# Another order of steps in an attention pipeline, and the output layer's first sums one product later

## The chip, the cores and the metric

The kernel runs on one core of one Trainium2 chip. The metric is the device time of one execution in microseconds (us); the time before is 1461.8 us, the median of 3 runs (1461.47 to 1461.99). The profile was taken of one further execution, whose span is 1460.0 us with a mean granted TensorE clock of 1.000.

## What is computed

```python
# attention: batch 8, heads 8, seq 576, head_dim 64; q, k, v in fp32
scores = scale * np.matmul(q, k.transpose(0, 1, 3, 2))           # scale = 1/8
thresh = np.max(scores, axis=-1, keepdims=True) - tau
scores = np.where(scores >= thresh, scores, -1e9)
attn = np.exp(scores - max); attn = attn / (sum(attn) + 1e-9)    # (shortened)
attn_out = np.matmul(attn, v)
# bridge: (B, H, S, D) -> (B*S, H*D), 4608 tokens of 512
# feed-forward: d_model 512, d_ff 2048
h = np.maximum(x @ w_in, 0.0)
out = h * h @ w_out
```

## The kernel before

**Attention.** The 64 heads are worked two at a time (32 pairs). A pair has five blocks of query rows: t = 0 to 3 with 128 rows of each head, t = 4 with the last 64 rows of both heads side by side. So there are 160 blocks, numbered n = 5i + t. They run through a software pipeline: in `slot(n)` the scores of block n+3 are computed, the softmax of n+2 and n+1 goes on, the weights of block n-1 are transposed, and the value products of block n-2 are made. `slot` only sets the order in which instructions are given to the engines; every engine then takes its own in that order.

```python
def ahead(n, part):                      # scores of block n, in two parts
    i, t = slots[n]
    if part == 0:
        jobs[n] = scores_rest(i, t)      # K: one 128x128 product (t < 4), takes one of 2 score tiles
    else:
        scores(i, t, jobs[n])            # S: 64-row products, the two heads on two halves of the array
        jobs[n] = softmax(i, t, jobs[n])

def softmax(i, t, sc):                   # a generator: stage(n) and second(n) each run one step
    ...
    for j in range(nj):                  # nj = 2, or 1 for t = 4
        nc.vector.tensor_reduce(out=nmx[:, j : j + 1], in_=sc[:, ds(at[j], S)], axis=AXIS.X, op=ALU.max, negate=True)
        ...                              # after the last: threshold on GpSimd
        yield
    for j in range(nj):
        if j:
            yield
        nc.scalar.activation(out=w[:, ts(j, S)], in_=sc[:, ds(at[j], S)], func=AF.Exp, bias=nmx[:, j : j + 1], scale=1.0)
    for j in range(nj):
        yield
        nc.vector.scalar_tensor_tensor(  # mask, multiply, sum; last reader of the score tile
            out=w[:, ts(j, S)], in0=sc[:, ds(at[j], S)], scalar=thr[:, j : j + 1], in1=w[:, ts(j, S)],
            op0=ALU.is_ge, op1=ALU.mult, accum_out=sm[:, j : j + 1])
    nc.gpsimd.tensor_scalar(out=sm[:, 0:nj], in0=sm[:, 0:nj], scalar1=1e-9, scalar2=None, op0=ALU.add)
    yield
    nc.vector.reciprocal(out=sm[:, 0:nj], in_=sm[:, 0:nj])
    ...                                  # normalize on GpSimd

def bank(shape, name):                   # two PSUM banks, given out in turn
    return b_pool.tile(shape, FP32, tag="b", name=name)        # b_pool has bufs=2

# the three parts of transposes(n): "R", "W" and "w"
def rest():                              # R: the rest columns, into the bank of the value products just made
    pt, n_, of = pending.popleft() if pending else (bank([P, 3, P], "pvR"), 0, None)
    nc.tensor.transpose(pt[:, 1, :], w[:, ds(MAIN, P)], ident[:, :])
    then = turn_last(i + 1, pt[:, 2, :]) if t == 0 and i + 1 in turning else None
    ...
    nc.scalar.copy(xr[:, :, :], pt[:, 0:2, :])     # copies value products and rest out of the bank
    ...                                  # then(): two more ScalarE copies and two GpSimd copies

def main(j):                             # W: j = 0, w: j = 1 (w does nothing for t = 4)
    if j and t == FULL:
        return
    pt = bank([P, FULL, P], "pwT")
    for c in range(FULL):
        nc.tensor.transpose(pt[:, c, :], w[:, ds(j * (S + REST) + c * P, P)], ident[:, :])
    ...
    nc.scalar.copy(wT[:, j, :, at], pt[:, :, :])

def values(i, t):                        # V: 64-column products, the two heads on two halves
    pt = bank([P, 3, P], "pvR")
    ...
```

`turn_step(n, 0)` (q) and `turn_step(n, 1)` (k) transpose the queries and the keys of the next pair, four transposes each into a `bank`; they act only in blocks with n mod 5 = 0. Blocks -1 to 34 and 75 to 110 also convert weights from 64-bit floats (`fetch`, `convert1` to `convert6`); `sums_step` makes one GpSimd sum of weights.

**Feed-forward.** Both layers are 49 products of blocks in place of 64 (two nested levels of a seven-product scheme). `OUTER` is the order of the outer products m; inside each, `inner` makes seven inner products with a `tick` after each. Sums of operands are made beside the products of other groups: on GpSimd, or on DVE with one operand copied to PSUM by ScalarE (`sum_v`). In the last step of the hidden layer, `work` holds the sums that the output layer needs first:

```python
OUTER, INNER = (1, 2, 6, 7, 4, 5, 3), (1, 6, 2, 7, 5, 4, 3)

def also(m, at):                         # called at each tick; i is the place of m in OUTER
    ...
    spread(work.get(i, []), at)          # one product's list, spread over its seven ticks

def inner_sums(n, m):                    # sums 5, 6, 3 on GpSimd, 7 on DVE
    return [lambda o=o: inner_g(n, m, o) for o in (5, 6, 3, 7)]

def sum_v(op, out, x, y):
    c = banks.tile([P, BANK], FP32, tag="c", bufs=2, name="c")
    ...
    nc.scalar.copy(c, y)
    return lambda: op(nc.vector, out, x, c)
```

The order of `slot`, before, is the first part of the diff below.

Of the kernel before, what the change touches and what calls it, by code (L numbers as in the profile page):

```python
# [48 lines left out]
def kernel(  # L49
# [26 lines left out]
    B, H, S, D = q.shape  # L76
# [133 lines left out]
    def convert3(m):  # L210
        if m not in parts:
            return
        a = parts[m][2].bitcast(FP32)
        low, high = (0x38000000, 0x47EFFFFF)
        nc.gpsimd.tensor_scalar(
            out=a, in0=a, scalar1=as_float(high), scalar2=as_float(low), op0=ALU.min, op1=ALU.max
        )

    def convert4(m):
        if m not in parts:  # L220
            return
        lo, hi, a = parts[m]
        nc.vector.tensor_scalar(
            out=a, in0=a, scalar1=3, scalar2=0x3FFFFFFF, op0=ALU.logical_shift_left, op1=ALU.bitwise_and
        )
# [224 lines left out]
    def turn_part(n, part):  # L450

        if n < 0:
            return
        if n not in rows_of:
            transposes(n)
        rows_of[n][part]()
# [33 lines left out]
    def turn_step(n, at):  # L490
        i, left = divmod(n - TURN_AT[at], NB)
        i += 1
        if left == 0 and 0 < i < len(pairs):
            if at == 0:
                turns[i] = turn(i)
            next(turns[i])

    def values_and_load(n):

        if n < 0:  # L500
            return
        i, t = slots[n]
        values(i, t)
        if t == NB - 1:
            turned.pop(i), loaded_v.pop(i)
            if i + 2 < len(pairs):
                load_v(i + 2)
# [3 lines left out]
    def stage(n):  # L511
        if n in jobs:
            next(jobs[n], None)

    def second(n):

        if n in jobs and slots[n][1] < FULL:
            next(jobs[n], None)
# [15 lines left out]
    IN_FIRST = OUT_SUMS + 41  # L534
# [4 lines left out]
    def sums_step():  # L539
        while summing and next(summing[0], 0) == 0:  # L540
            summing.popleft()

    def ask():

        while later:
            to, from_ = later.popleft()
            nc.sync.dma_start(out=to, in_=from_)
# [7 lines left out]
    def begun(n):  # L555
        return starts.get(n)

    def slot(n):

        sums_start(n)  # L560
        ask()
        turn_part(n - 1, "w")
        convert4(begun(n - 3))
        convert3(begun(n - 2))
        stage(n + 2)
        turn_step(n, 0)
        values_and_load(n - 2)
        convert1(begun(n - 1))
        stage(n + 1)
        second(n + 1)  # L570
        turn_part(n - 1, "R")
        second(n + 2)
        sums_step()
        turn_part(n - 1, "W")
        convert6(begun(n - 4))
        stage(n + 2)
        second(n + 2)
        fetch(begun(n + 3))
        convert5(begun(n - 3))
        ahead(n + 3, 0)  # L580
        stage(n + 1)
        turn_step(n, 1)
        ahead(n + 3, 1)
        convert2(begun(n - 1))


    def inner(product, copy, temp, bank, final, tick):
# [297 lines left out]
    with tc.manual_schedule():  # L885
        with ExitStack() as stack:
            sc_pool = stack.enter_context(tc.tile_pool(name="sc", bufs=2, space=PSUM))
            b_pool = stack.enter_context(tc.tile_pool(name="b", bufs=2, space=PSUM))

            def bank(shape, name):  # L890
                return b_pool.tile(shape, FP32, tag="b", name=name)

            def keep_busy(times):

                pt = bank([P, P], "idle")
                for _ in range(times):
                    nc.tensor.transpose(pt[:, :], ident[:, :], ident[:, :])

            load(0)
            load_v(0)  # L900
            keep_busy(10)
            for _ in turn(0):
                pass
            turn_last(0, bank([P, P], "pqkr")[:, :])()
            load_v(1)
            for n in range(-3, len(slots)):
                slot(n)
                if -3 < n < 0:
                    keep_busy(12)
                if n == IN_FIRST - 12:  # L910
                    load_x(0)
                    xsums = prepare_x(0, lambda op, out, x, y: op(nc.gpsimd, out, x, y))
                if n > IN_FIRST + 1 and n % 3 == 0:
                    next(xsums, None)
            n = len(slots)

            def drain():

                while pending:
                    pt, m, of = pending.popleft()  # L920
                    xr = sb.tile([P, 2, P], FP32, tag="xr", bufs=3)
                    nc.scalar.copy(xr[:, 0, 0:m], pt[:, 0, 0:m])
                    give_x(of, xr)

            drain()
            values_and_load(n - 2)
            for part in "RWw":
                turn_part(n - 1, part)
            values_and_load(n - 1)
            drain()  # L930
            for _ in range(60):
                sums_step()
            ask()
        banks = ctx.enter_context(tc.tile_pool(name="banks", bufs=1, space=PSUM))

        def reload(at):

            m, k = OUTER[at // 7], INNER[at % 7]
            t = weight_tile(W_OUT, m, k)
            nc.sync.dma_start(out=t[:, :], in_=w_dram[m, k][:, :])  # L940

        for n in range(NSTEP):
            last = n == NSTEP - 1
            if not last:
                load_x(n + 1)
                xsums = prepare_x(n + 1, sum_v)
            else:
                load_g(0, [(m, k) for m in (7, 4, 1, 2) for k in K_ORDER])
                rest = lambda: None
                first, second_one = outer_sums(0, 5, (1, 2))  # L950
                work = {
                    2: outer_sums(0, 5, (7,)) + outer_sums(0, 6, (7,)),
                    3: outer_sums(0, 3, (7,)) + outer_sums(0, 7, (7,)),
                    4: inner_sums(0, 1),
                    6: [rest, rest, first, rest, second_one, rest, rest],
                }

            def also(m, at):
                i = OUTER.index(m)
                if not last:  # L960
                    if 2 <= i <= 5 and at < 6:
                        next(xsums)
                    return
                spread(work.get(i, []), at)
                if 7 * i + at > 9:
                    reload(7 * i + at - 10)

            hidden_layer(n, also)
            if not last:
                next(xsums, None)  # L970
        for n in range(NSTEP):
            more = n + 1 < NSTEP

            def work_of(i):

                work = [] if i == 6 else inner_sums(n, OUTER[i + 1])
                if (n, i) == (0, 0):
                    work += outer_sums(0, 6, (1, 2)) + outer_sums(0, 5, (4,)) + outer_sums(0, 6, (4,))
                if (n, i) == (0, 1):
                    work += outer_sums(0, 7, (1, 2, 4)) + outer_sums(0, 3, (1, 2, 4))  # L980
                if more and i == 4:
                    work += outer_sums(n + 1, 5)
                if more and i == 5:
                    work += outer_sums(n + 1, 6) + outer_sums(n + 1, 7, (7, 1))
                if more and i == 6:
                    work += outer_sums(n + 1, 3) + outer_sums(n + 1, 7, (2, 4)) + inner_sums(n + 1, 1)
                return work

            def also(m, at):
                i = OUTER.index(m)  # L990
                if n == 0 and 7 * i + at < 10:
                    reload(39 + 7 * i + at)
                if more and (i, at) == (2 if n == 0 else 0, 0):
                    load_g(n + 1, [(m_, k) for m_ in KINDS[0:2] for k in K_ORDER])
                if at == 0:
                    work[0] = work_of(i)
                spread(work[0], at)
                if at > 4:
                    squares_due(0)
                if at == 2:  # L1000
                    ask()
                if at == 6:
                    if more and i == (2 if n == 0 else 0):
                        load_g(n + 1, [(7, k) for k in K_ORDER])
                    if more and i == (2 if n == 0 else 1):
                        load_g(n + 1, [(4, k) for k in K_ORDER])

            work = [None]
            output_layer(n, also)
        ask()  # L1010
# [36 lines left out]
```

## Time and profile before

| | before |
|---|---|
| time, median of 3 | 1461.8 us |
| span of the profile | 1460.0 us |
| PE (matmul) busy | 1435.8 us |
| PEld (weight load) busy | 1216.0 us |
| DVE busy | 1007.1 us |
| ACT busy | 890.8 us |
| POOL busy | 1053.6 us |
| hidden layer products (L708) | 396.6 us, 3528 |
| output layer products (L843) | 396.6 us, 3528 |
| attention transposes (L439) | 180.9 us, 1152 |
| value products (L469) | 163.3 us, 2560 |
| scores (L355) | 184.5 us, 768 |

PE is the matrix engine, PEld its weight loads, DVE the vector engine, ACT the scalar engine, POOL GpSimd. A line of the profile's groups or timeline names a source line (L439), the operation, what it writes and reads, and how often; times are start and duration in us. A bracket at the end of a line is idle time of that engine just before, and what ended it. Busy times of matmuls overlap and their ends are modelled, so distances from start to start say more than busy shares. The lines to know are L340 (rest scores K), L355 (scores S), L366 (maximum), L378 (exponential), L383 (mask), L439 (transposes W and w), L414 (rest transpose R), L418 to L427 (copies of R and V), L469 and L474 (value products V), L306 (q and k), L317 (last transpose of the next pair), L654 (copy of an operand for `sum_v`), L687 and L688 (squares).

### The profile page before, as it was taken

The numbers are of one execution on the slowest core, as the hardware profiler recorded it, in microseconds if no ns is written. First come the engines' busy times: TensorE is split into PE (matmuls) and PEld (weight loads), VectorE is DVE, ScalarE is ACT, GpSimd is POOL, SyncE is SP. The second block draws the span as 40 slices with busy tenths as digits, with TensorE's granted clock in tenths as the row PEclk, the third lists the DMA queues.
The fourth block names the chain that finished last, engine by engine and source line by source line (L and its number), as shares of the span: only waits on it lengthen the run. The fifth ranks groups of instructions, "written<-read, shape, count | busy, mean of one in ns | idle before, by whom it ended". The sixth has DMA issues, their size and how long they took to land. (4 is left out here: it accounts for less than half of the span.)

```text
span 1460.0 us, 35321 instructions
## 1 busy us (share of the span) xinstructions
PE 1435.8 (98%) x12914; PEld 1216.0 (83%) x12914; DVE 1007.1 (69%) x2152; ACT 890.8 (61%) x1792; POOL 1053.6 (72%) x1318
## 2 busy tenths in 40 slices
PE   8999999999999999999999999999999999999998
PEld 5666666666666666669999999999999999999998
DVE  4888766777887667666777877778765656545663
ACT  5888777778887777774766666767543333323330
POOL 3777788778888888773556655666777777777775
PEclk9999999999999999999999999999999999999999
DMA  4443223676442222202433233433984442244411
GB/s 126 106 129 109 66 65 115 189 229 183 122 123 75 54 54 65 64 26 63 145 124 132 94 109 123 146 123 119 387 303 146 145 131 78 89 138 145 145 30 30
DMA packets 212957, 176.90 MB, mean 121 GB/s; under 512 B 99888, under 2 KB 161328, under 8 KB 212784
## 3 DMA queue, kind: packets, MB, share of 16 engines
q1 hardware_dynamic: 210896, 174.09, 38.0%
q8 instruction: 102, 1.67, 0.5%
q10 hardware_dynamic: 1888, 0.56, 0.2%
q14 instruction: 71, 0.58, 0.1%
HBM read 105.12 MB, written 69.47 MB: 120 GB/s over the span
## 5 line engine op out<-in xcount | busy, mean ns | idle before, releaser
L133 POOL TENSOR_TENSOR arena<-arena 128x512 f32<-128x512 f32 (+1 forms) x314 | 376.8, 1223 | 250.4 <-DVE arena L133 221.1
L708 PE MATMUL ph<-arena,w 128*128 128x128 f32 x3528 | 396.6, 275 | 1.5 <-DVE arena L133 0.5
L708 PEld LDWEIGHTS ph<-arena,w 128*128 128x128 f32 x3528 | 394.7, 192 | 3.4 <-DVE arena L133 2.9
L843 PE MATMUL po<-w,arena 128*128 128x128 f32 x3528 | 396.6, 275 | 0.3
L843 PEld LDWEIGHTS po<-w,arena 128*128 128x128 f32 x3528 | 394.9, 192 | 2.0 <-issue 1.6
L133 DVE TENSOR_TENSOR arena<-ph,arena 128x512 f32<-128x512 f32 x378 | 255.4, 688 | 93.0 <-PE ph L708 52.3
L366 DVE TENSOR_REDUCE arena<-sc 128x1 f32<-128x576 f32 x288 | 217.6, 756 | 127.9 <-PE sc L355 127.7
L383 DVE SCALAR_TENSOR_TENSOR arena<-sc,arena 128x576 f32<-128x576 f32 x288 | 224.6, 814 | 7.2 <-ACT arena L378 6.9
L398 POOL TENSOR_SCALAR arena<-arena 128x576 f32<-128x576 f32 (+1 forms) x320 | 223.6, 709 | 7.4 <-DVE arena L389 2.6
L133 DVE TENSOR_TENSOR arena<-po,arena 128x128 f32<-128x128 f32 x378 | 108.2, 290 | 169.5 <-PE po L843 168.3
L654 ACT COPY c<-arena 128x512 f32<-128x512 f32 (+1 forms) x303 | 172.9, 580 | 62.9 <-DVE arena L130 56.8
L378 ACT ACTIVATE arena<-sc,arena 128x576 f32<-128x576 f32 x288 | 200.6, 746 | 10.7 <-DVE arena L366 6.4
L439 PEld LDWEIGHTS pwT<-ident,arena 128*128 128x128 f32 x1152 | 128.6, 141 | 76.1 <-issue 29.9
L355 PE MATMUL sc<-arena 64*128 64x512 f32 (+2 forms) x768 | 184.5, 571 | 1.1 <-DVE arena L383 0.7
L130 POOL TENSOR_TENSOR arena<-arena 128x512 f32<-128x512 f32 (+1 forms) x138 | 175.0, 1268 | 9.7
L439 PE MATMUL pwT<-ident,arena 128*128 128x128 f32 x1152 | 180.9, 280 | 0.5 <-ACT arena L441 0.3
L130 DVE TENSOR_TENSOR arena<-arena,c 128x512 f32<-128x512 f32 (+1 forms) x267 | 174.9, 663 | 7.5 <-ACT c L654 6.6
L441 ACT COPY arena<-pwT 128x512 f32<-128x512 f32 x256 | 151.5, 592 | 42.0 <-PE pwT L439 31.7
L469 PE MATMUL pvR<-arena 128*64 128x128 f32 (+1 forms) x2560 | 163.3, 268 | 5.1 <-ACT arena L441 0.7
L469 PEld LDWEIGHTS pvR<-arena 128*64 128x64 f32 x2560 | 127.8, 136 | 34.8 <-issue 20.8
L687 ACT ACTIVATE arena<-arena 128x512 f32<-128x512 f32 x144 | 90.0, 625 | 76.8 <-POOL arena L133 76.7
L622 ACT COPY arena<-po 128x128 f32<-128x128 f32 x63 | 16.7, 265 | 179.0 <-PE po L843 177.1
(56 smaller groups left out, 1158.1 us busy)
## 6 DMA issues: line engine op xcount, KB each, us to landing
g<-arena SPq DMA_DIRECT2D x144, 256.0 KB, 2.0
arena<-g SPq DMA_DIRECT2D x144, 256.0 KB, 4.5
w<-w SPq DMA_DIRECT2D x98, 256.0 KB, 4.9
out_dram<-arena SPq DMA_DIRECT2D x70, 128.0 KB, 2.3
arena<-in_q_dram SPq DMA_DIRECT2D x64, 128.0 KB, 2.7
arena<-in_v_dram SPq DMA_DIRECT2D x32, 256.0 KB, 2.8
arena<-in_moe_w_out_dram SPq DMA_DIRECT2D x16, 512.0 KB, 4.2
xT<-arena SPq DMA_DIRECT2D x128, 64.0 KB, 1.6
```

What stands on the lines that cost most here:

```text
L130: e.tensor_tensor(out=out, in0=x, in1=y, op=ALU.subtract)
L133: e.tensor_tensor(out=out, in0=x, in1=y, op=ALU.add)
L355: nc.tensor.matmul(to, qT[rows, ds(t * P, m)], kT[rows, ds(k0, n)], start=True, stop=True)
L366: nc.vector.tensor_reduce(out=nmx[:, j : j + 1], in_=sc[:, ds(at[j], S)], axis=AXIS.X, op=ALU.max, negate=True)
L378: nc.scalar.activation(out=w[:, ts(j, S)], in_=sc[:, ds(at[j], S)], func=AF.Exp, bias=nmx[:, j : j + 1], scale=1.0)
L383: nc.vector.scalar_tensor_tensor(out=w[:, ts(j, S)], in0=sc[:, ds(at[j], S)], scalar=thr[:, j : j + 1], in1=w[:, ts(j, S)], op0=ALU.is_ge, ...
L398: nc.gpsimd.tensor_scalar(out=out, in0=w, scalar1=r, scalar2=1.0, op0=ALU.mult, op1=ALU.mult)
L439: nc.tensor.transpose(pt[:, c, :], w[:, ds(j * (S + REST) + c * P, P)], ident[:, :])
L469: nc.tensor.matmul(pv[rows, :], va[:, j, c, :], wT[:, j, c, 0:n], start=(c == 0), stop=False, skip_group_check=True)
L654: nc.scalar.copy(c, y)
L708: nc.tensor.matmul(to[:, j, :], W_IN[m, k][:, ts(j, P)], of[k][:, m - 1, :], start=(not more and j == 0), stop=True, skip_group_check=True,)
L843: nc.tensor.matmul(to, g[:, j, :], w[:, j, :], start=(not more and j == 0), stop=(j == 3), skip_group_check=True)
```

## The change

Blocks in which no weights are converted (n = -3 and -2, 35 to 74, 111 to 159) take another order of steps: value products directly behind the scores, then all transposes R, w and W together, and k after the scores. The purpose is fewer changes between the shapes in which TensorE works. Blocks with conversion keep the old order. Three things come with it that put back an arrangement of the feed-forward: the first load of columns of x is issued 12 blocks later, three groups of sums for the output layer move by one product, and one more sum is made in the hidden layer's last product.

```diff
--- before.py
+++ after.py
@@ -555,33 +555,44 @@
     def begun(n):
         return starts.get(n)
 
+
+    ORDERS = ("LXMqVORwYWKEANBCDSeQfFGk", "LwCBXqVFMORYQWAEefDKNkSG")
+
+    def converting(n):
+
+        return any(begun(n - d) is not None for d in range(-1, 5))
+
     def slot(n):
 
         sums_start(n)
-        ask()
-        turn_part(n - 1, "w")
-        convert4(begun(n - 3))
-        convert3(begun(n - 2))
-        stage(n + 2)
-        turn_step(n, 0)
-        values_and_load(n - 2)
-        convert1(begun(n - 1))
-        stage(n + 1)
-        second(n + 1)
-        turn_part(n - 1, "R")
-        second(n + 2)
-        sums_step()
-        turn_part(n - 1, "W")
-        convert6(begun(n - 4))
-        stage(n + 2)
-        second(n + 2)
-        fetch(begun(n + 3))
-        convert5(begun(n - 3))
-        ahead(n + 3, 0)
-        stage(n + 1)
-        turn_step(n, 1)
-        ahead(n + 3, 1)
-        convert2(begun(n - 1))
+        steps = {
+            "L": lambda: ask(),
+            "w": lambda: turn_part(n - 1, "w"),
+            "C": lambda: convert4(begun(n - 3)),
+            "B": lambda: convert3(begun(n - 2)),
+            "X": lambda: stage(n + 2),
+            "q": lambda: turn_step(n, 0),
+            "V": lambda: values_and_load(n - 2),
+            "F": lambda: convert1(begun(n - 1)),
+            "M": lambda: stage(n + 1),
+            "O": lambda: second(n + 1),
+            "R": lambda: turn_part(n - 1, "R"),
+            "Y": lambda: second(n + 2),
+            "Q": lambda: sums_step(),
+            "W": lambda: turn_part(n - 1, "W"),
+            "A": lambda: convert6(begun(n - 4)),
+            "E": lambda: stage(n + 2),
+            "e": lambda: second(n + 2),
+            "f": lambda: fetch(begun(n + 3)),
+            "D": lambda: convert5(begun(n - 3)),
+            "K": lambda: ahead(n + 3, 0),
+            "N": lambda: stage(n + 1),
+            "k": lambda: turn_step(n, 1),
+            "S": lambda: ahead(n + 3, 1),
+            "G": lambda: convert2(begun(n - 1)),
+        }
+        for step in ORDERS[converting(n)]:
+            steps[step]()
 
 
     def inner(product, copy, temp, bank, final, tick):
@@ -907,7 +918,7 @@
                 slot(n)
                 if -3 < n < 0:
                     keep_busy(12)
-                if n == IN_FIRST - 12:
+                if n == IN_FIRST:
                     load_x(0)
                     xsums = prepare_x(0, lambda op, out, x, y: op(nc.gpsimd, out, x, y))
                 if n > IN_FIRST + 1 and n % 3 == 0:
@@ -946,13 +957,11 @@
                 xsums = prepare_x(n + 1, sum_v)
             else:
                 load_g(0, [(m, k) for m in (7, 4, 1, 2) for k in K_ORDER])
-                rest = lambda: None
-                first, second_one = outer_sums(0, 5, (1, 2))
                 work = {
-                    2: outer_sums(0, 5, (7,)) + outer_sums(0, 6, (7,)),
-                    3: outer_sums(0, 3, (7,)) + outer_sums(0, 7, (7,)),
-                    4: inner_sums(0, 1),
-                    6: [rest, rest, first, rest, second_one, rest, rest],
+                    3: [*outer_sums(0, 5, (7,)), *outer_sums(0, 6, (7,))],
+                    4: [*outer_sums(0, 3, (7,)), *outer_sums(0, 7, (7,))],
+                    5: inner_sums(0, 1),
+                    6: outer_sums(0, 5, (1, 2)) + outer_sums(0, 7, (1,)),
                 }
 
             def also(m, at):
@@ -977,7 +986,7 @@
                 if (n, i) == (0, 0):
                     work += outer_sums(0, 6, (1, 2)) + outer_sums(0, 5, (4,)) + outer_sums(0, 6, (4,))
                 if (n, i) == (0, 1):
-                    work += outer_sums(0, 7, (1, 2, 4)) + outer_sums(0, 3, (1, 2, 4))
+                    work += outer_sums(0, 7, (2, 4)) + outer_sums(0, 3, (1, 2, 4))
                 if more and i == 4:
                     work += outer_sums(n + 1, 5)
                 if more and i == 5:
```

## The prediction

> **What bounds the kernel now.** I read the page first: engine shares, then the chain of work that ended last.
>
> ```profile
> PE 1435.8 (98%) x12914; PEld 1216.0 (83%) x12914; DVE 1007.1 (69%) x2152; ACT 890.8 (61%) x1792; POOL 1053.6 (72%) x1318
> PE 27%; DVE 0%; issue 0%; DVEq 0%
> ```
>
> TensorE (PE) is busy 98% and the chain runs back through it for 27% of the span, to 1056.8 us, where a DVE addition interrupts it. The granted clock is 1.0. But a mean over the span hides two halves: the table of stretches gives weight loads 395 us of 399 in the hidden layer (about 660 to 1059 us), so nothing but fewer products would shorten that, while between 142 and 342 us, in the attention, they fill only 131 of 200 us. There PE's matmul time is full of changeovers. So I read the attention one PE group at a time, from the timeline filtered to PE. One block (n = 54, mod 5 = 4):
>
> ```profile
> 234.02 1.13 PE L355 MATMUL sc<-arena 64*128 64x512 f32 x4
> 235.08 0.66 PE L439 MATMUL pwT<-ident,arena 128*128 128x128 f32 x4
> 235.67 1.10 PE L469 MATMUL pvR<-arena 128*64 128x128 f32 x16
> 236.60 0.39 PE L474 MATMUL pvR<-arena 128*64 128x128 f32 x4
> 236.92 0.33 PE L414 MATMUL pvR<-ident,arena 128*128 128x128 f32 x1
> 237.09 0.60 PE L439 MATMUL pwT<-ident,arena 128*128 128x128 f32 x4
> 237.55 0.49 PE L340 MATMUL sc<-arena 128*128 128x128 f32 x2
> 237.97 1.13 PE L355 MATMUL sc<-arena 64*128 64x512 f32 x4
> ```
>
> Read start to start: scores S 1.06, second transposes w 0.59, value products V 0.93 + 0.32 = 1.25, rest transpose R 0.17, first transposes W 0.46, rest scores K 0.42. Sum 3.95. Four transposes inside a run cost 0.43 to 0.44 (0.108 apiece), so the 0.59 of w holds about **0.16 of changeover** to the 128x64 shape. The pattern repeats every five blocks. By block number mod 5, S to S: 3 is 3.82, 4 is 3.95, 0 is 4.49 (no w, and two groups of four transposes q and k of the next pair's queries and keys), 1 is 3.46 to 3.47 (narrow V, no K), 2 is 4.28. Sum 20.0 us for five blocks. The last pair of heads has no q and k, so one block of the kernel before already goes from S straight into V:
>
> ```profile
> 640.24 1.13 PE L355 MATMUL sc<-arena 64*128 64x512 f32 x4
> 641.30 1.10 PE L469 MATMUL pvR<-arena 128*64 128x128 f32 x16
> 642.55 0.33 PE L414 MATMUL pvR<-ident,arena 128*128 128x128 f32 x1
> 642.72 0.60 PE L439 MATMUL pwT<-ident,arena 128*128 128x128 f32 x4
> 643.70 0.49 PE L340 MATMUL sc<-arena 128*128 128x128 f32 x2 [0.39 <-DVE arena L383]
> 644.12 1.13 PE L355 MATMUL sc<-arena 64*128 64x512 f32 x4
> ```
>
> S to V takes the same 1.06 as S to w: one changeover either way. And the 0.39 in brackets is what happens when PE gets ahead: K waits for DVE's mask (L383), because the score tile has two buffers. The DVE side of block 54:
>
> ```profile
> 235.20 0.76 DVE L366 TENSOR_REDUCE arena<-sc 128x1 f32<-128x576 f32 x1 [1.39 <-PE sc L355]
> 235.93 0.82 DVE L383 SCALAR_TENSOR_TENSOR arena<-sc,arena 128x576 f32<-128x576 f32 x1
> 236.67 0.82 DVE L383 SCALAR_TENSOR_TENSOR arena<-sc,arena 128x576 f32<-128x576 f32 x1
> 237.41 0.76 DVE L366 TENSOR_REDUCE arena<-sc 128x1 f32<-128x576 f32 x1
> ```
>
> So there is a **second loop** beside PE's own: S, 1.18 later the first maximum, then two masks, and K 3.46 (block 155) to 3.53 (block 54) after S started; with K's 0.42 that makes 3.88 to 3.95. Block 54 sits on both loops at once: saving PE time there alone can bring 0.07 at most.
>
> **What the skill says.** "TensorEngine Tiling (Array Packing)", section Tiling Modes (Key Properties): changing the tiling mode drains the TensorE. The trace agrees: about 0.16 to 0.2 between the 128x128, 128x64 and 64x128 groups, none between w, W and R. "Perfetto Trace Analysis", section Tensor Engine Instruction: matmul ends in a trace are estimated; so I use starts only. "PSUM — Partial Sum Buffer", section Engine vs sequencer instructions: ScalarE, VectorE and GpSimdE queues are strict FIFO, and matmuls keep program order. The trace fits: a waiting ScalarE copy holds back all that follows (below).
>
> **The change, part by part.** It covers blocks 35 to 74 and 111 to 159: 89 blocks, 17.8 periods (two more at the start, before the pipeline fills).
>
> (a) Removed: w between S and V. In blocks 1 to 4 (mod 5) w joins R and W, one changeover less: 0.16. In block 1 k now stands between S and V, so it is not saved there. Three blocks of five: 3 x 0.16 = 0.48 per period, 17.8 x 0.48 = **8.5 us** at most if nothing waits.
>
> (b) Added: a buffer wait. There are two one-bank PSUM buffers, given out in turn. Old order w, V, W: W takes the bank of w, which V gave 1.25 us to be copied out. New order V, w, W: W takes the bank of V and R, and must wait for ScalarE's copy of R. That copy starts 0.37 after R:
>
> ```profile
> 237.29 0.37 ACT L418 COPY arena<-pvR 128x256 f32<-128x256 f32 x1 [0.87 <-PE pvR L414]
> ```
>
> so it ends at R + 0.74, and W can start at about R + 0.79 (0.05 from a ScalarE end to the PE start is what the tail after block 159 shows). Without the wait W would stand at R + 0.17 + 0.43 = R + 0.60. The wait is 0.19, more than the 0.16 removed, and I allow up to 0.07 for weights no longer loaded ahead. In block 1 R's bank also holds the next pair's last transpose, and four copies follow:
>
> ```profile
> 225.50 0.21 ACT L421 COPY arena<-pvR 128x64 f32<-128x64 f32 x1 [0.65 <-PE pvR L317]
> 225.98 0.23 ACT L321 COPY arena<-pvR 128x64 f32<-128x64 f32 x1
> ```
>
> R began at 225.03, the last copy ends 226.21: W at R + 1.23 in place of R + 0.71, a wait of 0.5.
>
> (c) Moved: k from before S to after it in block 0. S of that block comes 0.58 sooner; the 0.59 is paid in block 1.
>
> Walking five blocks with these numbers, S start to S start, W to S being 0.75 where nothing waits:
> - block 3: 1.06 + 1.25 + 0.79 to 0.86 + 0.75 = 3.85 to 3.92, call it 3.90 (was 3.82)
> - block 4: the same on PE, DVE's loop 3.88: 3.90 (was 3.95)
> - block 0: 1.06 + q 0.59 + 1.25 + R 0.17 + W 0.44 + K 0.41 = 3.92 (was 4.49)
> - block 1: 1.06 + k 0.59 + narrow V 0.73 + 1.22 + W to S 0.62 = 4.22, with the weight load 4.25 (was 3.46)
> - block 2: DVE sets it, through the exponentials that follow block 1's W; they stand as before against S: 4.04 if the first mask waits for its own exponential, 4.20 if for both as in the trace (was 4.28)
>
> Sum 20.01 to 20.17 against 20.0: 17.8 x 0 to 0.17 = 0 to +3 us. I take **+1 us**, leaning to the low end because old and new are so close and block 4 shows that PE's time there is not the last word.
>
> (d) Output layer's first sums: three groups move one product later, one DVE sum more stands in the last product of the hidden layer. ScalarE copies one operand of each, in its FIFO with the squares. The stretch is already full, and the one PE stall of that place comes from it:
>
> ```profile
> 1056.13 0.58 ACT L654 COPY c<-arena 128x512 f32<-128x512 f32 x1
> 1056.81 0.69 DVE L133 TENSOR_TENSOR arena<-arena,c 128x512 f32<-128x512 f32 x1 [1.07 <-POOL arena L133]
> 1058.15 1.16 PE L708 MATMUL ph<-arena,w 128*128 128x128 f32 x8 [0.47 <-DVE arena L133]
> ```
>
> GpSimd gets three sums of 1.28 into the product where it has six additions already (9 x 1.26 = 11.3 us of work in a product of 6.3), so the squares, and the copies behind them, come up to 2.5 us later. PE has six banks of slack. I estimate **+1 us** (0 to +3).
>
> (e) The load of the first columns 12 blocks later: still two blocks (8 us) ahead of its first user, against a median landing under 5 us for the page's DMA rows. Zero.
>
> Sum: 1461.8 + 1 + 1 = 1463.8; I say **1463.5**.
>
> **Rivals.** *Changeovers win:* if W doesn't wait (the copy of R ends sooner than I think), five blocks are 3.66 + 3.90 + 3.92 + 3.71 + 4.04 = 19.2, 17.8 x 0.8 = 14 us less: 1450. For it: 0.16 is plainly visible. Against: two buffers and a copy at R + 0.37. *DVE's loop takes all of it:* then blocks 3 and 4 tie at 3.9 and the result is within 2 us of before. Block 155's 0.39 speaks for it. *Waits win:* W waits on ScalarE behind other copies, and hidden-to-output stalls grow: +5 us attention, +3 us there, 1470.
>
> **Range and chances.** The attention spans -9 to +5 about its zero, the output layer 0 to +3: 1453 to 1470. Two per cent is 29 us, twice any rival, so within 2% has 0.97.
>
> **What would show it.** Timeline of PE after: V directly after S; w and W together; before W a wait on ScalarE L418 of about 0.2, in block 1 about 0.5. K's wait on DVE L383 should appear in block 4 or 0. Block 0 shorter by 0.57, block 1 longer by 0.8. Around 1057 us: DVE waiting for c, a PE gap over 0.7. I am wrong if W follows w without a gap (then the time falls towards 1450), or if the five-block period moves by over 0.3.

## The result and the profile after

| | before | after |
|---|---|---|
| time, median of 4 runs | 1461.6 us (1461.4 to 1462.0) | 1469.8 us (1469.2 to 1470.8) |
| ratio | | 1.0057, 95% interval 1.0039 to 1.0074 |
| span of the profile | 1460.0 us | 1468.0 us |

The changed kernel is 8.2 us slower: inside the range, close to its upper end, and on the side of the third rival (waits win). No busy time of the page grew by more than 0.4 us (DVE, from 1007.1); the span grew by 8.0:

```profile
PE 1435.5 (98%) x12914; PEld 1215.1 (83%) x12914; DVE 1007.5 (69%) x2152; ACT 890.1 (61%) x1792; POOL 1051.3 (72%) x1318
```

So the time is in gaps. The timeline of PE, for block 54 again:

```profile
234.50 1.13 PE L355 MATMUL sc<-arena 64*128 64x512 f32 x4
235.56 1.10 PE L469 MATMUL pvR<-arena 128*64 128x128 f32 x16
236.49 0.39 PE L474 MATMUL pvR<-arena 128*64 128x128 f32 x4
236.81 0.33 PE L414 MATMUL pvR<-ident,arena 128*128 128x128 f32 x1
236.98 1.28 PE L439 MATMUL pwT<-ident,arena 128*128 128x128 f32 x8
238.10 0.41 PE L340 MATMUL sc<-arena 128*128 128x128 f32 x2
238.44 1.13 PE L355 MATMUL sc<-arena 64*128 64x512 f32 x4
```

V stands directly behind S, and w and W stand in one row (x8). But eight transposes at 0.11 need 0.87, and K follows after 1.12. The group is merged, so the gap inside it is read from single starts: W stands 0.63 after w in place of 0.43. ScalarE's side names the wait, in the timeline first and then in the list of waits summed over the kernel (engine, line, what it waited for, us in total, times, longest):

```profile
237.18 0.37 ACT L418 COPY arena<-pvR 128x256 f32<-128x256 f32 x1 [0.88 <-PE pvR L414]
```

```profile
PEld pwT L439 <- ACT arena L418: 14.2, 54, 0.3
PEld pwT L439 <- ACT arena L321: 9.9, 17, 0.6
PE pwT L439 <- ACT arena L321: 5.9, 17, 0.4
```

The copy begins 0.37 after R (236.81) and W waits for it 54 times; in block 1 (mod 5) W waits for the last of four copies (L321) 17 times. Neither wait was there before. One more new wait, of ScalarE for a store (2.8 us, once, in block 80), is taken up below.

By block number mod 5, mean over blocks 45 to 69, S to S:

| block mod 5 | before | predicted | after |
|---|---|---|---|
| 0 | 4.49 | 3.92 | 3.92 |
| 1 | 3.46 | 4.25 | 4.19 |
| 2 | 4.28 | 4.04 to 4.20 | 4.22 |
| 3 | 3.82 | 3.90 | 3.91 |
| 4 | 3.94 | 3.90 | 3.94 |
| five blocks | 20.00 | 20.01 to 20.17 | 20.19 |

Counted along the two traces, the 8 us fall in these places: +1.4 from block 34 to 74 and +1.4 from 110 to 154 (the new order), +1.9 in one step at block 80, +1.5 between block 156 and the hidden layer, and +2.5 where the hidden layer ends, of which 0.3 comes back early in the output layer. The rest, -0.4, is spread over the start and the hidden layer.

### The profile page after: what moved, and what is told of

Its sections match the earlier page's. It is cut to its first block, busy times and chain, and to the rows that moved or that the text cites. A ratio compares the mean times of both kernels' runs of the same rounds, so it can differ in the third digit from the quotient of the medians.

```text
span 1468.0 us, 35286 instructions
## 1 busy us (share of the span) xinstructions
PE 1435.5 (98%) x12914; PEld 1215.1 (83%) x12914; DVE 1007.5 (69%) x2152; ACT 890.1 (61%) x1792; POOL 1051.3 (72%) x1318
## 5 line engine op out<-in xcount | busy, mean ns | idle before, releaser
L439 PE MATMUL pwT<-ident,arena 128*128 128x128 f32 x1152 | 181.1, 280 | 8.4 <-ACT arena L321 5.9
L439 PEld LDWEIGHTS pwT<-ident,arena 128*128 128x128 f32 x1152 | 128.5, 141 | 60.1 <-ACT arena L418 14.2
L441 ACT COPY arena<-pwT 128x512 f32<-128x512 f32 x256 | 151.2, 591 | 32.8 <-PE pwT L439 18.0
```

## Experiments

### The three parts alone

**The order of steps alone.** Load and sums as before (shown against the changed kernel; the lists of sums, also put back, are left out here):

```diff
-                if n == IN_FIRST:
+                if n == IN_FIRST - 12:
                     load_x(0)
```

> Only the new order of steps; the load of x and the output layer's first sums stay as before. Main theory (three separate costs, read from the two traces): -0.5 us at the start, 17 periods of five blocks at +0.16 to 0.18 each = +2.8, and +1.5 in the last three blocks, where V now stands directly behind w and W and waits for their copies: 1461.6 + 3.8 = 1465.4 us. Rival A (the order is the whole cost, the other two moves are hidden): 1469.8. Rival B (the order gains, as meant, by three changeovers in five blocks, and the other two parts cost more than the 8 us): below 1461.

Measured: 1466.0 us against 1461.8 (ratio 1.0029, 1.0018 to 1.0039), +4.2. Block lengths are those of the table above to 0.01; the steps are +1.4, +1.4 and +1.5 at the end. The 0.5 at the start is not found again (0.0 here). In block -1 the other runs' traces stand anywhere from 1.1 ahead of the trace of before to 0.3 behind it, so it was most likely such an offset.

**The load alone,** the kernel before with `n == IN_FIRST` for the load:

> The kernel before, with only the first load of x issued in block 76 in place of 64. Main theory: the issue queue is behind (stores of weight sums and loads of the next pair), the load is issued some 7 us late and lands 7 us after that, GpSimd's first sum of x waits for it and holds back the small GpSimd step that DVE's reciprocal needs: +1.9 us in one place (block 79 to 80), 1463.5 us. Rival A and my prediction's term (hidden): 1461.6.

Measured: 1463.9 us (1.0015, 1.0008 to 1.0022), +2.1; in the trace it is one step, of 1.8, at block 80.

**The sums alone,** the kernel before with the new lists of `work`:

> The kernel before, with only the output layer's first sums moved. Main theory: ScalarE's copies for the sums stand behind squares that wait for GpSimd, which has three more sums of 1.28 us in that product; DVE waits for the copies, PE for DVE: gaps of 1.4 and 2.1 us in place of 0.74 and 0.29, +2.4 us, 1464.0. Rival A: 1461.6, the gaps being a consequence of the changed attention. Prediction's term: +1.

Measured: 1464.0 us against 1461.8 (1.0017, 1.0010 to 1.0024), +2.2. The gaps of 1.4 and 2.1 us (from the start of one product to the start of the next, where the others stand 0.11 apart) are there with the attention untouched.

4.2 + 2.1 + 2.2 = 8.5 against 8.2 for the whole change: the parts add up within the spread of the runs. Both rivals fall: the order is not the whole cost, and it gains nothing.

**The order, but not in the last three blocks:**

```diff
-        for step in ORDERS[converting(n)]:
+        for step in ORDERS[converting(n) or n > 156]:
```

> As the first run, but the last three blocks (157 to 159), which have no scores, keep the old order. Main theory: w between R's run and V gives the copies time again: 1.5 us less than the first run, 1463.9. Rival: the three gaps before V are the drain of the pipeline itself and stay: as the first run, 1465.4.

Measured: 1464.5 us (1.0018, 1.0011 to 1.0026), 1.5 less than the order everywhere. Blocks 157 to 159 have no scores. There V directly behind W waits for W's copy (L441), which the timeline gives with the idle time in brackets; first the changed kernel, then this run:

```profile
654.62 1.28 PE L439 MATMUL pwT<-ident,arena 128*128 128x128 f32 x8
656.58 1.10 PE L469 MATMUL pvR<-arena 128*64 128x128 f32 x16 [0.68 <-ACT arena L441]
```

```profile
653.30 1.34 PE L439 MATMUL pwT<-ident,arena 128*128 128x128 f32 x8
654.58 1.10 PE L469 MATMUL pvR<-arena 128*64 128x128 f32 x16
```

In the second fence the x8 is W of one block and w of the next: w is work that fills the time of W's copy, and V follows 1.28 after the row began, in place of 1.96. The next block repeats it: V waits 0.73 at 660.01 in the changed kernel, and not at all at 657.33 in this run.

### Is it the copy behind R?

The size of that copy was changed in both directions. Made twice in the blocks without conversion, on the order-only kernel:

```diff
                 nc.scalar.copy(xr[:, :, :], pt[:, 0:2, :])
+                if 34 <= n <= 73 or n >= 110:
+                    nc.scalar.copy(xr[:, :, :], pt[:, 0:2, :])
```

> New order of steps only (as the first run, 1466.0), and the copy behind R made twice in the blocks without conversion: R's bank comes free about 0.3 us later. Theory 1 (W waits for the copy): W moves by 0.3 in blocks 2, 3 and 4 (mod 5); block 2 has 0.24 to spare before K, so +0.06, blocks 3 and 4 +0.3 each: 17 x 0.66 = +11 us, 1477. Theory 2 (DVE's loop has taken the gain, and the wait before W costs nothing): 1466 to 1467.

Measured: 1482.7 us against 1461.4 (1.0143, 1.0129 to 1.0157), 17 more than the order alone. W stands 1.03 after w (0.63 without). L420 is the second copy here, and the lines behind it move by two, so L439 is L441:

```profile
239.60 0.37 ACT L418 COPY arena<-pvR 128x256 f32<-128x256 f32 x1 [0.94 <-PE pvR L414]
240.00 0.37 ACT L420 COPY arena<-pvR 128x256 f32<-128x256 f32 x1
240.43 0.66 PE L441 MATMUL pwT<-ident,arena 128*128 128x128 f32 x4 [0.43 <-ACT arena L420]
```

The second copy ends at 240.37, W starts 0.06 later. Blocks 3 and 4 became 0.4 longer each, block 2 by 0.16. I had counted 0.3 a copy; the second one starts only when the first is done, so it is 0.4, and block 2's slack is used up. Theory 2 falls. The doubled copy was not run in the old order.

The short copy takes R's half only; value products of most blocks are left out of x, whose buffer is zeroed once:

```diff
-                nc.scalar.copy(xr[:, :, :], pt[:, 0:2, :])
+                nc.scalar.copy(xr[:, 1, :], pt[:, 1, :])
```

On the kernel before:

> The kernel before, but the ScalarE copy behind R takes only R's half of the bank (128x128, some 0.27 us, in place of 128x256, 0.37); the value products of most blocks are left out of x (their place in the buffer is set to zero once). Both theories (W waits for that copy in the new order only; or the loop through DVE sets the pace): in the old order nothing waits for this copy, 1461.8 +- 0.5 us. It is the control of the short copy in the new order.

Measured: 1461.1 us (0.9997, 0.9988 to 1.0005): no difference.

On the order-only kernel:

> New order only, with the short copy behind R (value products of most blocks left out of x). Theory 1: W about 0.1 sooner in blocks 2, 3, 4; block 3 gains 0.1, block 4 0.04 (then DVE's loop of 3.9 holds it), block 2 nothing (DVE holds it already): 17 x 0.14 = -2.4 us against the first run, 1463.6. Theory 2: no change, 1466.0.

Measured: 1463.1 us (1.0011, 1.0005 to 1.0018), +1.7 on before where the order alone had +4.2: 2.5 less. W stands 0.52 after w. Block 3 fell to 3.81, block 0 to 3.88, but block 4 stayed at 3.94, and its lines show why (all line numbers are two higher in this run):

```profile
237.07 1.18 PE L441 MATMUL pwT<-ident,arena 128*128 128x128 f32 x8
238.11 0.49 PE L342 MATMUL sc<-arena 128*128 128x128 f32 x2
238.53 1.13 PE L357 MATMUL sc<-arena 64*128 64x512 f32 x4
```

W ran 0.11 sooner, but K (L342) starts 3.52 after the block's S at 234.59, where the second loop puts it, and the next S follows 3.94 after the last, as without the short copy. There K's weight load already stood at 3.52 (238.02 in the changed kernel, whose S is at 234.50). So the wait for the copy is what the new order pays, in blocks that PE sets; in block 4, and in block 2, which stayed at 4.22, the loop through DVE holds whatever PE saves. The new order also gives some softmax steps another place in the queues of ScalarE and DVE; that was not tested apart.

### Does the moved k cost anything?

```diff
-    ORDERS = ("LXMqVORwYWKEANBCDSeQfFGk", ...
+    ORDERS = ("LXMqVORwYWKEANBCDkSeQfFG", ...
```

> New order only, but k stays between K and S in block 0 (mod 5), as in the old order. Theory 1 (the loss of blocks 0 and 1 together, +0.15 per five blocks, is the wait of block 1's W for the four copies behind R, not the moved k): block 0 back to 4.49, block 1 from 4.19 to about 3.61, time as the first run, 1466.0 +- 1. Rival (moving k costs a changeover that would otherwise be saved): block 1 falls to its old 3.46, 2.6 us less than the first run, 1463.4.

Measured: 1466.0 us against 1461.4 (1.0030, 1.0019 to 1.0041). Block 0 is 4.49 again, block 1 is 3.60, together 8.09 where the moved k had 8.11. Moving k shifts 0.58 from one block to the next and neither saves nor costs; the pair stays 0.14 above before because of W in block 1.

### Which of the sums, and can it be undone further?

Only the sums of the output layer's first product moved:

```diff
-                    4: inner_sums(0, 1),
+                    5: inner_sums(0, 1),
```

> The kernel before, with only the three GpSimd sums (and one on DVE) of the output layer's first product moved one product later. Theory (GpSimd is late in that product, so squares, copies, DVE and PE are late in turn): most of the +2.2 us of all moved sums, 1463.3. Rival (the further DVE sum in the last product, with its ScalarE copy, makes the gaps): 1461.5.

Measured: 1464.0 us against 1461.3 (1.0018, 1.0011 to 1.0025). Both gaps are there, from this one line:

```profile
1056.25 0.58 ACT L654 COPY c<-arena 128x512 f32<-128x512 f32 x1
1056.94 0.69 DVE L133 TENSOR_TENSOR arena<-arena,c 128x512 f32<-128x512 f32 x1 [1.74 <-ACT c L654]
1058.28 1.16 PE L708 MATMUL ph<-arena,w 128*128 128x128 f32 x8 [1.13 <-DVE arena L133]
...
1064.49 0.27 ACT L622 COPY arena<-po 128x128 f32<-128x128 f32 x1 [1.99 <-POOL arena L133]
1064.81 3.39 PE L843 MATMUL po<-w,arena 128*128 128x128 f32 x28 [1.80 <-ACT arena L622]
```

Read upward, the first gap: PE waits for DVE, DVE for ScalarE's copy c. The second: PE waits for ScalarE's copy of a product (L622), and that copy for a GpSimd sum. The rival (the further DVE sum) falls. The other way, on the kernel before:

```diff
-                    6: [rest, rest, first, rest, second_one, rest, rest],
+                    5: [rest, rest, rest, rest, rest, rest, first],
+                    6: [second_one] + 6 * [rest],
```

> The kernel before, with the two DVE sums of the hidden layer's last product moved the other way: the first to the end of the product before, the second to the first tick of the last. Theory (ScalarE's copies stand behind squares in its queue): the copies pass before the squares of that product, the gap of 0.74 us before the last hidden product goes, 0.6 us less: 1460.9. Rival (the gap is the load of DVE and ScalarE there, wherever the sums stand): the gap moves, 1461.5.

Measured: 1460.5 us against 1461.3 (0.9994, 0.9986 to 1.0002): the interval holds 1, so the time alone doesn't show a gain. The trace does show the mechanism, both gaps are gone, PE in one row to the layer's end and the next begun without idle time:

```profile
1049.77 8.70 PE L708 MATMUL ph<-arena,w 128*128 128x128 f32 x75
1058.31 5.88 PE L843 MATMUL po<-w,arena 128*128 128x128 f32 x51
```

Along the traces the stretch is 0.8 us shorter. Of the variants that leave nothing out it is the only one whose median lies below both kernels.

### Why the load costs 2 us

Two explanations stood: GpSimd's first sum of x (block 78) waits for data; or the load fills the DMA engines, and a store of x lands late, whose buffer ScalarE's copy behind R needs. First, the sums three blocks later (`n > IN_FIRST + 4`) with the load in block 76:

> Load of x in block 76 as in the second run (+2 us), and GpSimd's sums of x begin three blocks later (81). Theory 1 (GpSimd's sum waits for the load and holds all up): the loss goes, 1461.5. Theory 2 (a late store of x keeps the buffer that ScalarE's copy behind R needs, since the load fills the DMA engines): the loss stays, 1463.5.

Measured: 1462.6 us against 1461.3 (1.0010, 1.0002 to 1.0018), +1.3, and the step at block 80 is +2.2 in the trace (of an execution of 1463.4 us):

```profile
340.14 0.37 ACT L418 COPY arena<-pvR 128x256 f32<-128x256 f32 x1 [3.05 <-DMA xT<-arena]
340.57 0.66 PE L306 MATMUL pqk<-ident,arena 128*128 128x128 f32 x4 [1.40 <-ACT arena L418]
```

No sum waits for the load there (in the second run GpSimd had waited 2.0 us for it), ScalarE still waits 3.05 us for a store of x, and PE behind it. By time the loss is smaller than the +2.1 of the second run, but the intervals overlap; whether the sum has a part in it stays open. Second, the load in block 72 (`IN_FIRST - 4`):

> The kernel before, with the first load of x in block 72 in place of 64 (in block 76 it cost 2 us). Theory 1 (the first sum of x, in block 78, waits for the data: issue lag 7 us and landing 7 us): from block 72 it is there in time: 1461.5. Theory 2 (the load fills the DMA engines beside fetched weights, and a store of x, whose buffer the next copy needs, lands late): the first fetch is in block 73, so the collision is partly there: +1.

Measured: 1463.1 us (1.0012, 1.0004 to 1.0021), +1.8, with a step of +1.25 at block 75, before any sum, and ScalarE idle for a store again:

```profile
315.18 3.21 SPq L641 DMA_DIRECT2D arena<-xT  x4
318.48 0.41 SPq L547 DMA_DIRECT2D xT<-arena  x1
322.52 0.27 ACT L421 COPY arena<-pvR 128x128 f32<-128x128 f32 x1 [2.08 <-DMA xT<-arena]
```

So the late store carries the loss, and the first theory falls as an account of the whole. But full DMA engines are not the main reason why the store is late. SyncE (SPq) issues loads and stores one after the other, and this store (L547) stands behind the four parts of the load (L641). It is issued at 318.48, where the kernel before issued the same store at 315.17, and then lands 4.0 us later (before: 4.2). Here all of the delay is the issue; the DMA engines were full from 314 to 318 in both traces (101 and 103% by the profile). With the load in block 76 and the later sums, the store is issued 3.1 us later than before (335.58 and 332.50) and takes 2.1 us longer to land (4.5 and 2.4); in the two stretches of 4 us from 334 the engines are 92 and 96% busy. What makes block 64 harmless is open: it lies before the first fetch of weights (block 73), but there, too, the load is issued ahead of a store, and the engines are full for 8 us.

## Why the prediction was right or wrong

The range held, the sum was 6 us short. That it held is in part luck: 1469.8 lies 0.2 below its upper end, and the load's 2.1, a quarter of the loss, had no place in it. Step by step:

- **(a) right.** V follows S, the 0.16 of w is gone, S to V still takes 1.06.
- **(b) right in mechanism and nearly in size.** W at R + 0.80 was predicted as 0.79 to 0.86; in block 1 the wait is 0.52 (0.95 in place of 0.43), predicted 0.5. Both copy experiments confirm it.
- **(c) right:** 0.58 sooner, paid in block 1.
- **The attention's term was mis-sized.** The walk gave 0 to +0.17 a period, and I booked +1 us from the low end, because I let block 2's first mask wait for its own exponential alone (4.04). It is 4.22: the mask waits for both, as the trace of before already showed (in block 57 after, the second exponential ends at 248.57 and the mask begins at 248.67). The upper end, 0.17, was the measured one (0.19): about +2.8 us.
- **A term was missing.** The same order in the last three blocks, where no S fills the time of W's copy: +1.5. The walk covered only blocks with scores, and counted 157 to 159 as if they had them.
- **(d) right in mechanism, mis-sized:** +2.2 by time (+2.5 along the trace) where I put +1; the working had "up to 2.5 us later" for the squares and then let six banks of slack take all but 1. They did not: PE stood still 0.7 and 1.8 us longer than before.
- **(e) failed.** Zero was wrong, +2.1. The load was not two blocks ahead of its reader: with the load alone moved, its first part was issued at 332.42, 7.0 us after block 76's scores, behind other DMAs, and GpSimd waited 2.0 us for the data. And the question was only whether the load arrives in time, not what it delays: the store behind it, and with it ScalarE and PE.
- **The rivals:** "DVE's loop takes all of it" holds for blocks 4 and 2, not for block 3 (3.91 to 3.81 with the short copy). "Waits win" names the right kind of cause, but its 1470 is met by luck: +5 in the attention was +2.8 and +1.5 at its end, +3 at the sums was +2.2, and the load made up the rest. In blocks 2 to 4 W waits for R's own copy, not for one behind others. The 1450 of "changeovers win" is 1448 by its own numbers (1461.8 less 14), below the range.
- **The signs:** K's wait on DVE did not appear as a wait of its own (after: 3.3 us in 7 waits of PE; before: 5.7 us in 24). In block 4 it is covered by W: K's weight load at 238.02 follows DVE's mask, but W's transposes still run.

## What to carry to other kernels

Before two groups of work are put side by side to save a changeover, write down which buffer each takes and who frees it: a group that stood in between may have been the time in which a copy ran, and taking it away turns that copy into a wait of the same size. The same holds where a pipeline drains, since the steps that cover a copy are missing there. When a transfer is moved, ask which stores are issued behind it and which buffers those stores hold, not only whether its reader can wait.

## What was not expected of the hardware

Two copies in a row into the same place did not overlap: 0.40 from start to start (239.60 and 240.00 in the trace of the doubled copy) for 0.37 of duration, whereas the four different copies of block 1 start 0.11 to 0.21 apart. And a load of 1 MB in four parts, issued in 2 to 3 us, made a 64 KB store late enough to idle ScalarE for 2 to 3 us, in one run by its place in the order of issue alone (+3.3 us of issue, no longer landing).
